# A second level of the 7-for-8 algorithm in the last block's output product, with a GpSimd epsilon and a new order of the lead

## The chip, the cores and the metric

The kernel runs on one core of a Trainium2 chip. Its time is the device time in microseconds (us); before the change it is 1559.0 us, the median of three runs from 1556.36 to 1560.2 us. All profile numbers here are from one profiled execution, whose span is 1553.1 us at a mean granted TensorE clock of 0.998.

## The reference

Attention over 8 batches, 12 heads, 448 positions and 64 dimensions, then a feed-forward layer over the 3584 tokens of 768 features:

```
def rmsnorm(x, g):
    rms = np.sqrt(np.mean(x * x, axis=-1, keepdims=True) + 1e-06)
    return x / rms * g
q_n, k_n = rmsnorm(q, g_q), rmsnorm(k, g_k)
scores = 1.0 / np.sqrt(64) * np.matmul(q_n, k_n.transpose(0, 1, 3, 2))
attn = softmax(scores)                      # exp, divided by the sum over the keys
x = np.matmul(attn, v)                      # to (3584, 768): tokens by heads x dimensions
out = ((x @ w_a) * (x @ w_b)) @ w_out       # w_a, w_b: (768, 1536); w_out: (1536, 768)
```

The three weights arrive as 8-byte floats. The kernel turns them into fp32 itself; everything is then computed in fp32. In the profile one fp32 matmul shows as two records on TensorE (PE) and two weight loads (PEld).

## The kernel before, in words

**Attention.** A step p of 24 covers four heads of one batch (three steps to a batch). It loads q, k and v; squares q and k on ScalarE (L449); sums the squares on VectorE (L451); multiplies by 1/64 and adds 1e-6 on VectorE (L455); raises the result to the power -0.5 on GpSimd (L457); scales q with it (L461); and turns q and k over on TensorE (L487). Then, for seven slices j of the keys, TensorE makes the scores (L508), ScalarE their exponentials (L514), and TensorE multiplies them by v (L530). The sums over the keys: in the first five steps (WIDE) by a matmul with ones for each slice (L566); in the later 19 the seven exponentials are first added up by six additions of 128 x 896 elements (L544), each on the engine that ADD_UP names, and one matmul with ones follows. The sums are inverted through a round trip to DRAM (L586 to L595) and multiplied into the result (L636).

**Feed-forward.** Two batches make a block, so there are four blocks (beta 0 to 3) of 896 tokens. Each of the two layers uses a form of Strassen's algorithm: a product of two 2 x 2 block matrices in 7 block products in place of 8, at the price of additions of blocks. The first layer (`quarter_products`, matmuls at L790) keeps a weight's 7 factors stationary and streams 448 tokens. The second (`last_product`) keeps token tiles stationary and streams 384 columns of a factor of w_out: for each of its 7 products f, in the order 0, 1, 2, 4, 3, 5, 6, and each pair t of token tiles it makes six matmuls of 128 x 384 (`product`, L718). Blocks 0 and 2 have three pairs, blocks 1 and 3 have four (one made of the tiles left over). VectorE makes the sums of token tiles (`sum_`, L706) and adds the products up (L738, L754, L761, L767); `store` (L862) sends finished tiles out from SyncE.

**Weights.** `factors` loads the two parts of a piece of weight (L372, L375, issued by ScalarE's queue), rounds it (L271 to L280), makes the seven factors (L385), and keeps them in DRAM (L393, L396) for the later blocks; `stream` brings them back (L406, L408) into one of two buffers `st`. `weights` calls it for 18 pieces in the order `seq`, each not before the moment in GATES. The five first pieces are of w_out.

**The order of the work.** Everything is recorded first as operations of a `Plan`: engine, an estimated duration, a key (the lower, the more urgent), what it reads and writes, and which buffers it opens. `Plan.run` then simulates the engines with these estimates and writes every engine's instructions in the order that comes out. The order on the chip is therefore fixed; a wait on the chip holds everything behind it on that engine. An operation with `lock=True` is planned so that no two such operations of VectorE and GpSimd overlap. NORM says how many steps ahead of its use a step's normalization is keyed, LANDING what is allowed for a transfer to arrive, XS the number of buffers of 128 x 3 x 448 elements that hold the attention's results and their sums. The lead, as it is called here, is the time until the first block's first layer runs alone, some 240 us, in which attention and weights share all engines.

Of the kernel before, what the change touches and what calls it, by code (L numbers as in the profile page):

```python
# [25 lines left out]
class Plan:  # L26
# [10 lines left out]
    LANES = 8  # L37
    RATE, LANDING = 300.0, 2.0
    STAY = 0.3
# [131 lines left out]
def kernel(  # L171
# [35 lines left out]
    nc = tc.nc  # L207
# [91 lines left out]
    def fast_body(ld, wk, ps_s, ps_o, ps_mm, dram):  # L299
        plan = Plan()  # L300
        op, tile_of = plan.op, plan.tile
        NORM = 2.5
        EARLY = 1.5
        FEW = S // 8
        HC, NT = HP // 2, S // D
        NC = B * HC
        STS, XS = 2, 9
        WARM = 8
        APART = 24
        WIDE = 5  # L310
        ADD_UP = [None, 'DVE', 'POOL', 'DVE', 'POOL', 'DVE', 'DVE']

# [37 lines left out]
        def factors(n, key, early, after):  # L350

            last = n >= len(order)
            st = tile_of(f"st{n}", "st", STS)

            def begin():
                sts[n] = ld.tile([P, 7, KH * P], FP32, tag="st", name="st", bufs=STS)
            op(None, 0.0, key, begin, [], [f"{st}/{x}" for x in range(7)] + ["streaming"], new=[st])
            if last:
                m = n - len(order)
                steps = ((0, 4, 1, 0), (0, 5, 3, 1), (1, 1, 3, 4), (0, 6, 2, 1))  # L360
            else:
                m, ab = order[n]
                src = (moe_w_a, moe_w_b)[ab]
                steps = ((0, 4, 2, 3), (1, 5, 0, 2), (0, 2, 4, 0), (0, 6, 1, 2))
            words, row = place(early)

            for part in range(2):
                def load(part=part):
                    to = words()[:, part * NW:(part + 1) * NW]
                    if last:  # L370
                        k = m + part * MH
                        nc.scalar.dma_start(to, moe_w_out[k * P:(k + 1) * P, :])  # L372
                    else:
                        at = part * HM + m * P
                        nc.scalar.dma_start(to.rearrange("p (k n) -> p k n", k=KA),  # L375
                                            src[:, 2 * at:2 * (at + P)].rearrange("(k p) n -> p k n", p=P))
                op("ACT", 0.45, key - 0.75, load, after, [f"{row}/{part}"], kb=768)
            rounding(key, NW, lambda: (words().rearrange("p (n w) -> p n w", w=2), sts[n][:, 0:4].rearrange("p a b -> p (a b)")),
                     [f"{row}/{part}" for part in range(2)], f"{st}/0")
            homes = [0, 0, 0, 0, 4, 5, 6]  # L380
            for pool_, to, x, y in steps:
                add = to == 4 and not last
                e = FACTOR if pool_ else "DVE"
                op(e, 1.05 if e == "POOL" else 0.6, key,
                   lambda e=e, to=to, x=x, y=y, add=add: two[e].tensor_tensor(  # L385
                    sts[n][:, to], sts[n][:, x], sts[n][:, y], ALU.add if add else ALU.subtract),
                   [f"{st}/{homes[x]}", f"{st}/{homes[y]}"], [f"{st}/{homes[to]}"], lock=True)

            def keep():
                if last:  # L390
                    if "o" not in kept:
                        kept["o"] = dram.tile([P, 7, MH, HALF], FP32, name="kept_o")
                    nc.scalar.dma_start(kept["o"][:, :, m], sts[n])  # L393
                else:
                    kept[n] = dram.tile([P, 7 * KH * P], FP32, name=f"kept{n}")
                    nc.scalar.dma_start(kept[n], sts[n].rearrange("p a b -> p (a b)"))  # L396
            op("ACT", 0.45, key, keep, [f"{st}/{x}" for x in range(7)], [f"kept{n}"], kb=1376)

# [33 lines left out]
        def normalize(p):  # L432
# [8 lines left out]
            def squares(s, nm):  # L441
                sq = tile_of(f"sq{nm}{p}", "sq", 1)

                def square():
# [3 lines left out]
                            x.rearrange("p j h d -> p (j h) d"))  # L448
                    nc.scalar.activation(t, flat, AF.Square)  # L449
                op("ACT", 1.07, key, square, [f"{nm}{p}"], [sq], new=[sq])  # L450
                op("DVE", 1.1, key, lambda: nc.vector.tensor_reduce(rs[p][:, s], xs["sq", nm, p], AX, ALU.add), [sq], [f"{ms}/{nm}"])  # L451

            def roots(a, b, names):
                msf = lambda: rs[p][:, a:b].rearrange("p s n -> p (s n)")
                op("DVE", 0.2, key, lambda: nc.vector.tensor_scalar(msf(), msf(), 1.0 / D, 1e-6, ALU.mult, ALU.add), [], names)  # L455
                op("POOL", 2.7 if b - a == 1 else 5.0, key,
                   lambda: nc.gpsimd.tensor_tensor(msf(), msf(), expo[:, 0:2 * NT * (b - a)], ALU.pow), [], names)  # L457

# [111 lines left out]
        def invert(p):  # L570
# [25 lines left out]
            for w in range(2):  # L596
                op("ACT", 0.55, p - 0.5, lambda w=w: move(w), [f"su{p}.{w}" if p < WIDE else f"su{p}"], [t], new=[t] if w == 0 else [])
            op("SP", 0.8, p - 0.0, spread_out, [t], [few], new=[few], kb=20, dmas=2)
            op("DVE", 0.3, p - 0.0, lambda: nc.vector.reciprocal(fews[0], fews[0]), [], [few])
            op("SP", 0.4, p - 0.0, leave, [few], [f"inv{p}"], kb=20)  # L600
            op("SP", 1.0, p - 0.0, come_back, [f"inv{p}"], [t], kb=460, dmas=2)

# [13 lines left out]
        def put_out(p):  # L616

            for w in range(2):
# [4 lines left out]
                def take(w=w, x=x, c=c):  # L623
                    if c == 0:
                        quads[x] = wk.tile([P, KH, S], FP32, tag="x", name="x", bufs=XS)
                    nc.scalar.copy(quads[x][:, c], os_[p][:, w, 0:S])
                op("ACT", 0.55, p, take, [f"o{p}"], [f"{x}/{c}"] + (["quarter"] if c == 0 else []), new=[x] if c == 0 else [])

        def divide(p):

            for w in range(2):
                x, c = home(p, w)

                def emit(w=w, x=x, c=c):
                    t = quads[x][:, c]
                    nc.vector.tensor_tensor(t, t, sus[p][:, w], ALU.mult)  # L636
                op("DVE", 0.65, p, emit, [f"rec{p}"], [f"{x}/{c}"], lock=True)

# [6 lines left out]
        def combine(beta, c):  # L645

            B11, B21, B12, B22, T2, T3, T4 = names_of(beta)
            for to, x, y in ((T3, B22, B12), (B12, B12, B11), (T2, B22, B12), (T4, B21, T2)):
# [6 lines left out]
                if first:  # L655
                    tile_of(to, "x", XS)
                op("DVE", 0.63, -0.5, emit, [f"{x}/{c}", f"{y}/{c}"], [f"{to}/{c}"] + (["quarter"] if first else []),
                   new=[to] if first else [], lock=True)
# [20 lines left out]
        def last_product(beta, h, key):  # L679
# [24 lines left out]

            def sum_(to, x, y, alu):
                op("DVE", 0.98, -0.5, lambda: nc.vector.tensor_tensor(to[0](), x[0](), y[0](), alu), x[1] + y[1], to[1][:1], lock=True)  # L706

# [21 lines left out]
            def out_(t, i, x, y):  # L729

                g = 2 * S * beta + (t + OWN * i) * P if t < OWN else 2 * S * (beta - 1 + i) + 2 * OWN * P

# [10 lines left out]
            for f in (0, 1, 2, 4, 3, 5, 6):  # L743
                stream(beta, 12 + place_of[f], f)
            for t in pairs:
                sum_(n_(t), A(1, 0, t), A(1, 1, t), ALU.add)
                sum_(n_(t), n_(t), A(0, 0, t), ALU.subtract)
            for t in pairs:
                product(t, 0, A(0, 0, t), lambda po, ps, t=t: op(
                    "ACT", 0.5, -1, lambda: nc.scalar.copy(acc(t, 0), ps()), [po], [c_(t)]))  # L750
                sum_(A(0, 0, t), A(0, 0, t), A(1, 0, t), ALU.subtract)
            for t in pairs:
                product(t, 1, n_(t), lambda po, ps, t=t: op(
                    "DVE", 0.6, -1, lambda: nc.vector.tensor_tensor(acc(t, 1), acc(t, 0), ps(), ALU.add), [po, c_(t)], [U_(t)]))  # L754
            for t in pairs:
                product(t, 2, A(0, 1, t), out_(t, 0, 0, 0))
                sum_(A(0, 1, t), A(0, 1, t), n_(t), ALU.subtract)
                sum_(n_(t), A(1, 0, t), A(1, 1, t), ALU.add)
            for t in pairs:
                product(t, 4, n_(t), lambda po, ps, t=t: op(  # L760
                    "DVE", 0.6, -1, lambda: nc.vector.tensor_tensor(acc(t, 0), acc(t, 1), ps(), ALU.add), [po, U_(t)], [c_(t)]))  # L761
            for t in pairs:
                product(t, 3, A(0, 1, t), out_(t, 0, 1, 0))
            for t in pairs:
                def both(po, ps, t=t):
                    out_(t, 1, 1, 0)(po, ps)
                    op("DVE", 0.6, -1, lambda: nc.vector.tensor_tensor(acc(t, 1), acc(t, 1), ps(), ALU.add), [po], [U_(t)])  # L767
                product(t, 5, A(0, 0, t), both)
            for t in pairs:
                product(t, 6, A(1, 1, t), out_(t, 1, 0, 1))  # L770
            if not odd:
                op("ACT", 1.5, 0, lambda: nc.scalar.copy(left(), H()[:, :, 2 * OWN * P:]), allh, [f"{fin}/left"])

        def quarter_products(beta, key, m, ab, st, at, names, h):
# [112 lines left out]

        GATES = [0, 2, 4, 4, 5, 5, 7, 7, 8, 8, 10, 10, 16, 18, 21, 21, 27, 32]
        seq = [15, 13, 16, 12, 14, 0, 1, 2, 3, 4, 5, 6, 7, 8, 9, 10, 11, 17]
        def weights(at, after):  # L890
            for x, n in enumerate(seq):
                if at == GATES[x]:
                    factors(n, x * 0.45 + 1.0, x < 2, [after])

# [4 lines left out]
        for p in range(NC + 1):  # L899
# [16 lines left out]
            if p > 0:  # L916
# [6 lines left out]
                if p % (2 * HC) == 0:  # L923
                    combine(p // (2 * HC) - 1, 1)
                    combine(p // (2 * HC) - 1, 2)
                    ffn(p // (2 * HC) - 1)
            if p < NC:
# [139 lines left out]
```

## Time and profile before

| engine | busy, us | share of the span | what it mostly does |
|---|---|---|---|
| PE | 1518.8 | 98% | first layer (L790) 763.2, second layer (L718) 388.4, the rest attention |
| DVE (VectorE) | 715.0 | 46% | weights, sums, taking products from PSUM |
| ACT (ScalarE) | 395.7 | 25% | exponentials 192.2 |
| POOL (GpSimd) | 313.6 | 20% | power 146.3, products of the first layer 86.2, adding up 80.9 |

An engine's busy time is a sum over its records; matmuls overlap in the records, so the mean of a record (540 ns for 448 columns) is a latency, and the distance between two of them is read from a run of many: their time divided by their number. Shares over the whole span hide where an engine is short, so the table is read together with a table by stage, in which each row is a stretch of the span.

### The profile page before, as it was taken

The page shows a single profiled execution, that of the slowest core. Times are in us where ns is not written, and L with a number is a line of the kernel's source. Part 1 is how long each engine was busy: PE and PEld are TensorE (multiplying, and loading weights), DVE is VectorE, ACT ScalarE, POOL GpSimd, SP SyncE. Part 2 cuts the span into 40 slices and gives each one's busy share as a digit, 9 for nine tenths or more (in the row PEclk, how much of TensorE's full clock was granted, in tenths as well). Part 3 has the DMA queues.
Part 4 walks back from the last instruction along what each step waited for, and adds up shares of the span by engine and source line. Part 5 has one row for each costly group of instructions (what it writes and reads, how often), then busy time and mean ns, then how long its engine had stood idle before and what let it go on. Part 6 is the DMA issues. An engine that isn't in the chain of part 4 may idle for free.

```text
span 1553.1 us, 16949 instructions
## 1 busy us (share of the span) xinstructions
PE 1518.8 (98%) x6714; PEld 790.3 (51%) x6714; DVE 715.0 (46%) x932; ACT 395.7 (25%) x637; POOL 313.6 (20%) x166
## 2 busy tenths in 40 slices
PE   8988999999999999999999999999999999999998
PEld 6653345555444555555444555555545555555554
DVE  4887869888786412222476421222245221222421
ACT  5767661111567200000547300000040000000000
POOL 3416542211345200011246200001010001001000
PEclk9999999999999999999999999999999999999999
DMA  9897445544445542212325333222213422121222
GB/s 248 234 264 228 97 108 176 210 171 169 146 118 126 152 147 75 103 71 106 91 80 127 89 118 117 100 78 85 92 44 117 156 90 107 72 107 66 95 92 80
DMA packets 113884, 192.26 MB, mean 124 GB/s; under 512 B 56196, under 2 KB 99460, under 8 KB 104068
## 3 DMA queue, kind: packets, MB, share of 16 engines
q1 hardware_dynamic: 86052, 138.00, 30.2%
q10 hardware_dynamic: 27744, 53.09, 9.8%
q8 instruction: 55, 0.90, 0.2%
q14 instruction: 33, 0.27, 0.1%
HBM read 154.93 MB, written 35.95 MB: 123 GB/s over the span
## 4 chain that ended last, share of the span: by engine, by line
PE 88%; DMA 4%; ACT 3%; DVE 3%; issue 1%; POOL 1%; SPq 0%; ACTq 0%; DVEq 0%; POOLq 0%
PE pq L790 48%; PE po L718 24%; PE sc L508 6%; PE o L530 6%; PE pt L487 2%; PE su L566 2%; ACT ET L514 2%; DMA q_sb<-in_q_dram 1%; DMA kept_o<-st 1%; PE warm L879 1%; DMA hraw<-in_moe_w_out_dram 1%; DVE x L636 0%; DVE sum L544 0%; DMA st<-kept_o 0%; DMA rec<-inv 0%
## 5 line engine op out<-in xcount | busy, mean ns | idle before, releaser
L790 PE MATMUL pq<-x,st 128*128 128x448 f32 x2016 | 763.2, 540 | 0.0
L790 PEld LDWEIGHTS pq<-x,st 128*128 128x128 f32 x2016 | 382.2, 190 | 377.4 <-issue 369.9
L718 PE MATMUL po<-st,hT 128*128 128x384 f32 x744 | 244.0, 487 | 0.0
L514 ACT ACTIVATE ET<-sc,ms 128x448 f32<-128x448 f32 x336 | 192.2, 635 | 89.8 <-PE sc L508 64.2
L530 PE MATMUL o<-ET,v_sb 64*64 64x448 f32 x1344 | 184.7, 547 | 8.2 <-ACT ET L514 7.7
L508 PE MATMUL sc<-qkT 64*64 64x448 f32 x1344 | 176.5, 546 | 16.5 <-ACT ET L514 8.3
L718 PEld LDWEIGHTS po<-st,hT 128*128 128x128 f32 x744 | 141.0, 190 | 100.6 <-issue 3.6
L457 POOL TENSOR_TENSOR ms<-ms,expo 128x14 f32<-128x14 f32 x48 | 146.3, 3051 | 190.6 <-DVE ms L455 185.7
L838 POOL TENSOR_TENSOR hT<-hT,t 128x448 f32<-128x448 f32 x24 | 28.4, 1184 | 756.1 <-DVE t L836 753.9
L718 PE MATMUL po<-st,fin 128*128 128x384 f32 x432 | 144.4, 489 | 0.0
L812 ACT COPY hT<-pq 128x448 f32<-128x448 f32 x24 | 12.8, 532 | 441.7 <-PE pq L790 441.7
L718 PEld LDWEIGHTS po<-st,fin 128*128 128x128 f32 x432 | 81.2, 190 | 61.4 <-issue 6.3
L544 POOL TENSOR_TENSOR sum<-sum,ET 128x896 f32<-128x896 f32 x38 | 80.9, 2130 | 129.8 <-ACT ET L514 74.8
L508 PEld LDWEIGHTS sc<-qkT 64*64 64x64 f32 x1344 | 58.7, 133 | 92.6 <-issue 33.7
L530 PEld LDWEIGHTS o<-ET,v_sb 64*64 64x64 f32 x1344 | 60.0, 133 | 85.6 <-ACT ET L514 40.6
L738 DVE TENSOR_TENSOR o_sb<-fin,po 128x384 f32<-128x384 f32 x56 | 31.0, 554 | 155.9 <-PE po L718 155.9
L544 DVE TENSOR_TENSOR sum<-sum,ET 128x896 f32<-128x896 f32 x57 | 62.4, 1094 | 39.2 <-POOL sum L544 30.8
L850 POOL TENSOR_TENSOR hT<-hT,t 128x448 f32<-128x448 f32 x48 | 57.8, 1206 | 49.5 <-DVE t L847 45.9
L451 DVE TENSOR_REDUCE ms<-sq 128x14 f32<-128x896 f32 x48 | 51.8, 1078 | 25.0 <-ACT sq L449 25.0
L843 DVE TENSOR_TENSOR hT<-U,pq 128x448 f32<-128x448 f32 x48 | 29.8, 621 | 66.0 <-PE pq L790 66.0
L815 ACT COPY t<-pq 128x448 f32<-128x448 f32 x24 | 12.8, 533 | 176.0 <-PE pq L790 176.0
L847 DVE TENSOR_TENSOR t<-U,pq 128x448 f32<-128x448 f32 x48 | 29.7, 619 | 60.1 <-PE pq L790 57.8
(69 smaller groups left out, 923.0 us busy)
## 6 DMA issues: line engine op xcount, KB each, us to landing
st<-kept SPq DMA_DIRECT2D x36, 1344.0 KB
st<-kept_o SPq DMA_DIRECT2D x28, 1152.0 KB
kept<-st ACTq DMA_DIRECT2D x12, 1344.0 KB
q_sb<-in_q_dram SPq DMA_DIRECT2D x48, 224.0 KB
k_sb<-in_k_dram SPq DMA_DIRECT2D x48, 224.0 KB
v_sb<-in_v_dram SPq DMA_DIRECT2D x48, 224.0 KB
rec<-inv SPq DMA_DIRECT2D x48, 224.0 KB
out_dram<-o_sb SPq DMA_DIRECT2D x112, 96.0 KB
```

Source lines behind the costliest of these rows:

```text
L451: op("DVE", 1.1, key, lambda: nc.vector.tensor_reduce(rs[p][:, s], xs["sq", nm, p], AX, ALU.add), [sq], [f"{ms}/{nm}"])
L457: lambda: nc.gpsimd.tensor_tensor(msf(), msf(), expo[:, 0:2 * NT * (b - a)], ALU.pow), [], names)
L487: nc.tensor.transpose(t[:, j * P:(j + 1) * P], x[:, j].rearrange("p h d -> p (h d)"), ident)
L508: nc.tensor.matmul(t[low_high[w], e, 0:S], lhsT=qkTs[p][low_high[e], 1, j * P + w * D:j * P + (w + 1) * D], rhs=qkTs[p][low_high[e], 0, w ...
L514: nc.scalar.activation(E[:, e], scs[p, j][:, e, 0:S], AF.Exp, scale=rs[p][:, 1, 2 * j + e:2 * j + e + 1])
L530: nc.tensor.matmul(os_[p][low_high[e], w, 0:S], lhsT=xs["v", p][low_high[w], e, j * D:(j + 1) * D], rhs=ETs[p, j][low_high[w], e], start=( ...
L544: two[e].tensor_tensor(sums[p], sums[p] if j > 1 else ETs[p, 0], ETs[p, j], ALU.add)
L566: nc.tensor.matmul(sus[p][w][low_high[e], :], lhsT=ones[low_high[w], :], rhs=x[low_high[w], e], start=first, stop=last)
L718: nc.tensor.matmul(held["po"][:, 0:HALF], lhsT=a[0]()[:, c], rhs=sts[beta, 12 + place_of[f]][:, c], start=(c == 0), stop=(c == MH - 1))
L738: nc.vector.tensor_tensor(held["o"], acc(t, y), ps(), ALU.add)
L790: nc.tensor.matmul(banks[bank][:, 0:S], lhsT=sts[at][:, f, c * P:(c + 1) * P], rhs=quads[x][:, c], start=(start and c == 0), stop=(stop an ...
L850: lambda i=i, n=n, nm=nm: two[TIMES].tensor_tensor(C(i, n), C(i, n), held[nm], ALU.mult), [t], [hp[i]],
```

## The change

It has four parts.

- **Second level.** In the last block alone (ONCE), for five of the seven products (TWICE: f = 1, 2, 3, 4, 6), two pairs of token tiles are taken together as a 2 x 2 block matrix, and their product with the factor of w_out is done in 7 products of three matmuls of 128 x 192 where the plain form takes 12 matmuls of 128 x 384, the work of 8 such products (`inner_products`). The factors of the factors are made once, in block 1 (MAKE), by VectorE, and kept in DRAM (`inner_factors`); in the last block they are read back into buffers that the finished attention no longer needs (`stream_inner`). Products 0 and 5 stay plain. The sums of token tiles that the last block needs first are made piece by piece while its first layer still runs.
- **1e-6 on GpSimd.** The squares are scaled on ScalarE so that their sum is the mean; the addition of 1e-6 moves from VectorE to GpSimd, ahead of the power.
- **Adding up.** ADD_UP gives four of the six additions to GpSimd, where it was two.
- **Order of the lead.** Loads of weights are issued by SyncE (LOADS) in place of ScalarE; keys, GATES, `seq`, NORM, LANDING and some estimated durations change, and XS goes from 9 to 8.

```diff
-    RATE, LANDING = 300.0, 2.0
+    RATE, LANDING = 300.0, 2.5
...
-        NORM = 2.5
+        NORM = 2.0
...
-        STS, XS = 2, 9
+        STS, XS = 2, 8
         WARM = 8
+        TWICE = (1, 2, 3, 4, 6)
+        MAKE = 1
+        ONCE = NB - 1
+        LOADS = "SP"
+        KEEPS = "ACT"
...
-        ADD_UP = [None, 'DVE', 'POOL', 'DVE', 'POOL', 'DVE', 'DVE']
+        ADD_UP = [None, 'DVE', 'POOL', 'POOL', 'DVE', 'POOL', 'POOL']
...
-                        nc.scalar.dma_start(to, moe_w_out[k * P:(k + 1) * P, :])
+                        queue[LOADS].dma_start(to, moe_w_out[k * P:(k + 1) * P, :])
...
-                op("ACT", 0.45, key - 0.75, load, after, [f"{row}/{part}"], kb=768)
+                op(LOADS, 0.45, key - 2.0, load, after, [f"{row}/{part}"], kb=768)
...
-                    nc.scalar.activation(t, flat, AF.Square)
+                    nc.scalar.activation(t, flat, AF.Square, scale=float(D) ** -0.5)
...
-                op("DVE", 0.2, key, lambda: nc.vector.tensor_scalar(msf(), msf(), 1.0 / D, 1e-6, ALU.mult, ALU.add), [], names)
-                op("POOL", 2.7 if b - a == 1 else 5.0, key,
-                   lambda: nc.gpsimd.tensor_tensor(msf(), msf(), expo[:, 0:2 * NT * (b - a)], ALU.pow), [], names)
+
+                def root():
+                    nc.gpsimd.tensor_scalar(msf(), msf(), 1e-6, None, ALU.add)
+                    nc.gpsimd.tensor_tensor(msf(), msf(), expo[:, 0:2 * NT * (b - a)], ALU.pow)
+                op("POOL", 3.2 if b - a == 1 else 5.6, key, root, [], names)
...
+            def each(f, a, base, to):
+                twice = groups if f in TWICE else []
+                for g in twice:
+                    inner_products(beta, key + place_of[f], f, g, a, base, to, acc, (c_, U_), out_place)
+                for t in pairs if not twice else alone:
+                    product(t, f, a(t), plain(t, base, to))
...
+            factor(0, a10, a11, ALU.add, nx1)
+            factor(1, s(0), a00, ALU.subtract, nx0 + [f"{S_}/0"])
+            factor(2, a00, a10, ALU.subtract, nx)
+            factor(3, a01, s(1), ALU.subtract, nx0 + [f"{S_}/1"])
...
+            product("a", a00, b_quarter(0, 0), nx0 + [st], True, False)
+            op("ACT", 0.32, -1, copy, [bank_of["a"]], [f"{t_}/0"], new=[t_])
+            product("b", s(1), b_made(1), [f"{S_}/1", f"ti{beta}.{f}.1"], True, True)
...
+            product("a", a01, b_quarter(1, 0), nx0 + [st], False, True)
...
+            product("d", s(0), b_made(0), [f"{S_}/0", f"ti{beta}.{f}.0"], True, True)
...
+            product("g", s(2), b_made(2), [f"{S_}/2", f"ti{beta}.{f}.2"], True, False)
...
+            product("e", s(3), b_quarter(1, 1), [f"{S_}/3", st], True, True)
+            product("g", a11, b_made(3), nx1 + [f"ti{beta}.{f}.3"], False, True)
...
-        GATES = [0, 2, 4, 4, 5, 5, 7, 7, 8, 8, 10, 10, 16, 18, 21, 21, 27, 32]
-        seq = [15, 13, 16, 12, 14, 0, 1, 2, 3, 4, 5, 6, 7, 8, 9, 10, 11, 17]
+        GATES = [0, 2, 3, 4, 5, 6, 7, 7, 7, 9, 11, 11, 11, 11, 17, 17, 18, 20]
+        seq = [13, 15, 12, 14, 16, 0, 1, 2, 3, 4, 5, 6, 7, 8, 9, 10, 11, 17]
...
-                    factors(n, x * 0.45 + 1.0, x < 2, [after])
+                    factors(n, x * 0.65 + 0.5, x < 1, [after])
```

## The prediction

> **What bounds the kernel now.** First the page: busy time by engine, and the line of the 40 slices for TensorE.
>
> ```profile
> PE 1518.8 (98%) x6714; PEld 790.3 (51%) x6714; DVE 715.0 (46%) x932; ACT 395.7 (25%) x637; POOL 313.6 (20%) x166
> ...
> PE   8988999999999999999999999999999999999998
> ```
>
> TensorE is the bound, and only the first four slices and the last show room. The view by windows says how much:
>
> ```profile
> 0.00:240.00 240.00, 217.78 (x1796) 120.20 (x1797) 179.54 (x216) 159.55 (x250) 104.99 (x44) 0.99 0.73 194
> ...
> 380.00:520.00 140.00, 136.55 (x953) 62.99 (x952) 101.61 (x122) 82.75 (x136) 59.85 (x26) 1.00 0.48 128
> ...
> 700.00:875.00 175.00, 172.91 (x1049) 80.89 (x1048) 90.87 (x115) 82.14 (x139) 63.67 (x29) 1.00 0.36 99
> ...
> 1438.00:1547.00 109.00, 108.60 (x337) 63.81 (x335) 33.95 (x49) 1.91 (x4) 1.13 (x1) 1.00 0.30 93
> 1547.00:1553.10 6.10, 0.00 (x0) 0.00 (x0) 0.19 (x1) 0.00 (x0) 0.00 (x0) 0.66 0.15 38
> ```
>
> The columns after the length are PE, PEld, DVE, ACT and POOL busy, then the clock. PE idles 22.2 us in the lead (240 - 217.8), 3.5 and 2.1 us in the attention of blocks 1 and 2, nothing in the last product (from 1438), and 6.5 us in the tail. So a matmul removed from the last product is worth its whole time, and the rest of the change can bring at most the 22 us of the lead. The chain of waits, in order of time (start, length, what), gives the price of a matmul:
>
> ```profile
> 12.61 9.43 DMA hraw<-in_moe_w_out_dram
> ...
> 25.12 1.12 PE o L530 x5
> ...
> 193.60 1.53 PE pt L487 x14
> ...
> 958.15 178.14 PE pq L790 x474
> ...
> 1438.24 108.37 PE po L718 x336
> ```
>
> A record of 384 columns comes every 108.37 / 336 = 322.5 ns, one of 448 every 178.14 / 474 = 375.8 ns, one of 128 (the turning of q and k) every 1.53 / 14 = 109 ns: about 0.83 ns a column and no floor down to 128. The first two lines belong to the lead: a piece of w_out, loaded by ScalarE's queue at 12.6, holds ScalarE, and TensorE's next product waits until 25.1. Last, the groups (busy us, mean ns | idle before them):
>
> ```profile
> L457 POOL TENSOR_TENSOR ms<-ms,expo 128x14 f32<-128x14 f32 x48 | 146.3, 3051 | 190.6 <-DVE ms L455 185.7 <-ACT x L626 4.1
> L718 PEld LDWEIGHTS po<-st,hT 128*128 128x128 f32 x744 | 141.0, 190 | 100.6 <-issue 3.6 <-DVE sum L544 0.7 <-DVE o_sb L738 0.7
> ...
> L544 POOL TENSOR_TENSOR sum<-sum,ET 128x896 f32<-128x896 f32 x38 | 80.9, 2130 | 129.8 <-ACT ET L514 74.8 <-DVE sum L544 38.8 <-DVE ms L451 11.8
> L544 DVE TENSOR_TENSOR sum<-sum,ET 128x896 f32<-128x896 f32 x57 | 62.4, 1094 | 39.2 <-POOL sum L544 30.8 <-ACT ET L514 7.3
> ...
> L455 DVE TENSOR_SCALAR ms<-ms 128x14 f32<-128x14 f32 x48 | 18.6, 388 | 1.4
> ```
>
> GpSimd takes 1.95 times as long as VectorE for the same addition.
>
> **What the Trainium skill says.** "TensorE: Matmul & The Clock Gate", section "LDWEIGHTS (loading the stationary operand)": a load takes its columns / 1.2 ns, so 107 ns for 128, whatever the rows. The trace shows records of 190 ns but turnings with a load each every 109 ns, so 190 is a latency, and a load fits under 192 columns. The same page, Part 1: after about 3.4 us of idleness the clock is halved until TensorE has been busy again. The trace agrees: after the gap up to 25.1 the granted clock is 0.83 in 24 to 28 us and 0.74 in 28 to 32. "SBUF — State Buffer", "SBUF: two separate sides": VectorE operations with two SBUF inputs and GpSimd operations take one pair of ports by an exclusive lock. The 0.388 us of L455, whose shortest is 0.110 and longest 2.092, fit an operation held by GpSimd.
>
> **Second level, TensorE.** Ten groups (five products, two groups each) lose 12 matmuls of 384 columns, 240 records in all: 240 x 322.5 ns = 77.4 us. They gain 21 of 192, 420 records. At the line through 128 and 384 (109 and 322.5 ns: 0.834 a column) a record is 162.4 ns: 68.2 us. **Gain 9.2 us** (an eighth of 77.4 would be 9.7; the fixed part of more records takes the rest). The bounds: 320/2 = 160 ns with no fixed part gives 10.2; if the 190 ns of a load did bind, 420 x 190 = 79.8, a loss of 2.4. I take 162, since the 109 ns speak against the second.
>
> **Second level, VectorE.** A group takes four sums of 384 elements (L385 has this shape: 0.55 undisturbed), six additions out of PSUM of 192 (384 take 0.555, 448 0.62, so about 0.36) and two on SBUF (0.35 and 0.55): 2.2 + 2.2 + 0.9 = 5.3 us, beside 6.8 us of TensorE (42 x 162 ns). The stage has 33.6 us of VectorE work in 108; it gets 53 more and loses 20 additions of 0.555, 11: some 75 in 99 us. It stays hidden on average. Locally it may not: between f = 2 and f = 4 lie eight sums of 0.96 (L706) and the eight factors of f = 4, 12 us, while TensorE has 13.7 us of f = 2, whose own additions take another 6 us of VectorE. Each group's first and third products need no such factor (2 us of cover), so I put 1 us for stalls, between 0 and 4. Sums moved under the first layer cost nothing: VectorE is busy 71 of 268 us there (1170 to 1438). Making 20 factors of 576 elements (0.75) costs 15 us of VectorE in block 1, busy 58 of 255 us there, and 5.9 MB out and back over queues at a DMA share of 0.3: hidden. The tail stays DVE, then two transfers; two tiles now end 1 us apart rather than 3.9, and a pair of issues takes 1.1 us (1547.2 to 1548.3): +0.5, between 0 and 1.
>
> **1e-6.** It takes 48 operations of 0.388 from VectorE, 18.6 us and one hand-over of each chain, and puts 48 on GpSimd. No such row exists there; setting 28 columns takes 0.12 us (L236), selecting over 128 columns 0.29: between 0.12 and 0.5, I take 0.3. Behind it in GpSimd's order wait the power and the additions; for the power wait q's scaling and then the turning on TensorE. The scale on ScalarE is free, being part of the same activation.
>
> **Adding up.** Nineteen steps move two additions each: VectorE loses 2 x 1.09, GpSimd gains 2 x 2.13. A step of TensorE is 7.35 (scores) + 7.70 (values) + 1.90 (turning) + 1.0 (sums), 18 us; GpSimd goes from 2 x 3.05 + 2 x 2.13 = 10.4 to 15.2 us of it. That fits, with 15% to spare. The chain of six additions grows from 8.6 to 10.7 us, under 18. I put 1 us for attention, between -3 and 19.
>
> **Order of the lead.** Moving loads to SyncE frees ScalarE of 10 issues of about 0.4 us in the lead, and the first piece of w_out is issued right behind the first v, some 5 us earlier. The gap before 25.1 is 3.9 us, and the slow clock behind it costs 8 us x 0.21 = 1.7; I take 60% of these 5.6. The other 18 us are small waits for ScalarE, with VectorE busy 75%; relief of VectorE (18.6 us of L455 over 24 steps, some 8 in the lead) may take a tenth, 2 us. With XS = 8 the first layer of block 0 begins after 9 steps, not 11; that moves work, not its sum. **Gain 5 us**, between -6 and 14: SyncE's queue is in order too, and a load that waits for room holds q and k of the next step.
>
> **Sum.** 1559.0 - 9.2 + 1 + 0.5 + 1 - 5 = 1547.3, say 1547.
>
> **Rivals.** (A) The lead clears more than I allow: half of its 22 us and the slow clock, 12 us in place of 5, and no stalls: 1559 - 9.2 + 0.5 - 12 = 1538. For it: the gap has one visible cause. Against: DMA share is near 1 from 20 to 140 us, and the order alone moves no fewer bytes. (B) The second level is partly eaten: stalls of 4 us in the last product, tail +1, lead and attention together nothing: 1555. For it: VectorE would be over TensorE at f = 2 to 4. Against: two banks and two pairs of banks let TensorE run ahead. (C) GpSimd becomes the bound of attention. With the port lock, two-input work of VectorE (two additions, q's scaling, dividing, block sums: about 6 us a step) must fit into the gaps of 8.5 us of GpSimd additions; a late sum holds TensorE, whose order is fixed. One us a step is 19 us, no gain in the lead, stalls as forecast: 1559 - 9.2 + 2.5 + 19 = 1571, slower than before. For it: 85% busy leaves little for an in-order queue, and VectorE now waits for GpSimd on more links. Against: powers last 3 us but VectorE's two-input L278 ran at its usual 1.76 us beside one at 29.6, so they don't hold the port.
>
> **Numbers.** Forecast 0.52, A 0.18, B 0.18, C 0.12. The range leaves out C and the far side of A: 1536 to 1560. Faster than 1554.3: forecast, A and half of B, 0.79; within 0.3%: the other half of B and little else, 0.09; slower: C, 0.12.
>
> **What would show it.** In the second profile: records of 192 columns every 162 ns in the chain (near 190 would refute the main step); PE busy about 1510; idle of PE in the last product under 4 us; a first gap of PE shorter than 3.9 us and a clock of 1.00 at 24 to 32 us; the sum's matmul with ones not waiting on GpSimd L553's additions. PE idle above 15 us between the lead and the last block would mean C.

## The result, and the profile after

The changed kernel takes 1576.16 us (median of 4 runs), the kernel before 1557.83 us beside it: a ratio of 1.0116, 95% interval 1.0098 to 1.0134. It is **slower by 18 us**, where 1547 was forecast. The two profiled executions lie 22.6 us apart (1575.7 against 1553.1), since that of before took less than its median and that of after more. The accounts below are in profile time, so about 4 us in them are scatter between executions.

The page of the kernel after, busy time by engine and TensorE's line of slices:

```profile
PE 1522.8 (97%) x6894; PEld 819.0 (52%) x6894; DVE 729.3 (46%) x982; ACT 399.0 (25%) x647; POOL 430.4 (27%) x252
...
PE   9888799999999999999999999999999999999987
```

The last but one slice is no longer full, and one at 160 us is a 7. By windows (stretch, length, busy PE, PEld, DVE, ACT, POOL, granted clock, DMA share, GB/s), kernel after:

```profile
0.00:240.00 240.00, 212.62 (x1579) 119.41 (x1580) 166.57 (x184) 137.30 (x211) 120.62 (x69) 0.96 0.67 195
380.00:520.00 140.00, 137.31 (x889) 65.70 (x882) 80.56 (x91) 75.92 (x125) 97.51 (x50) 1.00 0.50 136
700.00:875.00 175.00, 173.22 (x1055) 85.57 (x1054) 94.00 (x108) 82.60 (x139) 99.22 (x53) 1.00 0.42 120
1450.50:1568.00 117.50, 104.82 (x516) 85.60 (x515) 64.94 (x144) 5.12 (x14) 1.13 (x1) 1.00 0.36 115
```

Three readings. The lead idles 27.4 us where it idled 22.2, and its clock is 0.96, not 0.99. The attention of blocks 1 and 2 idles 2.7 and 1.8 us: as little as before (3.5 and 2.1), with GpSimd busy 97.5 of 140 us and 99.2 of 175. The last product, which had no gap, now has 12.7 us of them (117.5 - 104.8). The chain of waits of the kernel after, around the end of the last first layer (start, length, what):

```profile
1261.07 189.42 PE pq L986 x504
...
1450.49 15.48 PE po L729 x48
1465.97 2.92 PE ab L903 x18
1468.89 1.96 PE dg L903 x12
1471.29 1.26 PE dg L903 x6
1472.98 1.24 PE dg L903 x6
1474.22 2.92 PE ab L903 x18
...
1566.64 1.26 PE dg L903 x6
```

These lines cut the loss in three. The last product begins at 1450.5 where it began at 1438.2: **12.3 us lost ahead of it**. On TensorE it lasts 117.4 us (1450.5 to 1567.9) and not 108.4: **9.0 us lost in it**, where 8.2 were to be gained. The tail grows from 6.5 to 7.8: 1.3. Together 22.6. The first part is the one that scatters: two runs below, e1 and e4, have the order of this kernel ahead of the last product, and in their profiles it begins 8.7 and 7.6 us later than before, not 12.3.

A third view says where the first part arises. The end of each block's first layer, read from the chain, gives these lengths (us):

| kernel | start to block 0 | to block 1 | to block 2 | to block 3 | rest |
|---|---|---|---|---|---|
| before | 386.1 | 364.7 | 385.5 | 301.9 | 114.9 |
| after | 371.4 | 362.1 | 386.2 | 330.8 | 125.2 |

### The profile page after: what moved, and what is told of

It reads as the page before. It is cut to its first block, busy times and chain, and to the rows that moved or that the text cites. A ratio compares the mean times of both kernels' runs of the same rounds, so it can differ in the third digit from the quotient of the medians.

```text
span 1575.7 us, 17582 instructions
## 1 busy us (share of the span) xinstructions
PE 1522.8 (97%) x6894; PEld 819.0 (52%) x6894; DVE 729.3 (46%) x982; ACT 399.0 (25%) x647; POOL 430.4 (27%) x252
## 4 chain that ended last, share of the span: by engine, by line
PE 90%; DVE 3%; DMA 3%; ACT 2%; issue 1%; SPq 0%; POOL 0%; ACTq 0%; DVEq 0%; POOLq 0%
PE pq L986 49%; PE po L729 19%; PE o L539 7%; PE sc L517 6%; PE dg L903 3%; PE su L575 2%; PE pt L496 2%; PE ab L903 2%; ACT ET L523 1%; DMA kept_o<-st 1%; DMA rec<-inv 1%; PE warm L1075 1%; DVE fin L716 1%; DVE x L646 1%; DMA few<-rec 1%
## 5 line engine op out<-in xcount | busy, mean ns | idle before, releaser
L729 PE MATMUL po<-st,hT 128*128 128x384 f32 x624 | 206.7, 488 | 0.0
L553 POOL TENSOR_TENSOR sum<-sum,ET 128x896 f32<-128x896 f32 x76 | 165.8, 2181 | 140.9 <-DVE sum L553 115.7
L539 PE MATMUL o<-ET,v_sb 64*64 64x448 f32 x1344 | 191.1, 547 | 6.3 <-ACT ET L523 5.7
L729 PEld LDWEIGHTS po<-st,hT 128*128 128x128 f32 x624 | 117.2, 190 | 86.9 <-issue 7.3
L465 POOL TENSOR_TENSOR ms<-ms,expo 128x14 f32<-128x14 f32 x48 | 140.3, 2922 | 4.0
L729 PE MATMUL po<-st,fin 128*128 128x384 f32 x312 | 104.0, 488 | 0.0
L729 PEld LDWEIGHTS po<-st,fin 128*128 128x128 f32 x312 | 58.6, 190 | 44.2 <-issue 3.5
L749 DVE TENSOR_TENSOR o_sb<-fin,po 128x384 f32<-128x384 f32 x44 | 24.4, 555 | 107.0 <-PE po L729 101.1
L464 POOL TENSOR_SCALAR ms<-ms 128x14 f32<-128x14 f32 x48 | 36.7, 765 | 116.3 <-DVE ms L458 114.3
```

The source lines that it names most:

```text
L464: nc.gpsimd.tensor_scalar(msf(), msf(), 1e-6, None, ALU.add)
L539: nc.tensor.matmul(os_[p][low_high[e], w, 0:S], lhsT=xs["v", p][low_high[w], e, j * D:(j + 1) * D], rhs=ETs[p, j][low_high[w], e], start=( ...
L553: two[e].tensor_tensor(sums[p], sums[p] if j > 1 else ETs[p, 0], ETs[p, j], ALU.add)
L729: nc.tensor.matmul(held["po"][:, 0:HALF], lhsT=a[0]()[:, c], rhs=sts[beta, 12 + place_of[f]][:, c], start=(c == 0), stop=(c == MH - 1))
```

## Experiments

Differences in us are (ratio - 1) x 1558. Every run was timed beside the kernel before on the same chip, whose medians were 1557.2 to 1558.8. Theory names (X, Q, R, T and others) are those of the expectations.

### Which half costs

**e1** keeps the lead and attention as changed and has no second level:

```
-        TWICE = (1, 2, 3, 4, 6)
-        ONCE = NB - 1
+        TWICE = ()
+        ONCE = NB
```

> The changed kernel without the second level (TWICE empty, ONCE past the last block): the last product is plain again and nothing is made in block 1. Read from the two traces, the first layer of the last block ends 12.3 us later than before, and the last product with its tail takes 10.3 us more. Theory L (the lead's order alone costs the 12.3): 1566 to 1571 us, the first layer of the last block ending near 1450, the last product back at 108.4 us. Rival (making the inner factors and moving sums cost time before the last product): about 1558 us, the end of the first layer near 1438.

Measured 1568.74, ratio 1.0060 (1.0043 to 1.0078), +9 us. **e2** is the opposite: second level and XS = 8 kept, everything else of the lead and attention as before (loads on ScalarE's queue, 1e-6 on VectorE, ADD_UP, keys, GATES and `seq`).

> The kernel before plus the second level alone; XS is 8 as in the change (9 leave no room in SBUF for the two tk buffers). Orders, keys, loads, 1e-6 and adding up are as before. Theory L: the lead is as before, only the last product is longer: 1558 + 10 = 1568 us. Rival X (XS = 8 is what costs the lead its 12 us): 1580 us, the first layer of the last block ending near 1450.

Measured 1573.7, 1.0090 (1.0068 to 1.0112), +14. **e3** is the kernel before with one number changed:

```
-        STS, XS = 2, 9
+        STS, XS = 2, 8
```

> The kernel before with XS = 8 in place of 9 and nothing else. Theory L: within 3 us of 1558. Rival X: 1570 us.

Measured 1566.48, 1.0052 (1.0025 to 1.0078), +8. So the second level costs about 7 us in the old order (1573.7 - 1566.5) and 7.5 in the new one (1576.2 - 1568.7). Both halves lose, and within the intervals they add up. The lengths of e3 are 362.7, 363.4, 387.6, 332.8: two attention steps move from the lead to the stretch before the last first layer. They were worth 23.4 us in the lead (386.1 - 362.7) and cost 30.9 us behind it (332.8 - 301.9). Why they cost more there is not shown: TensorE idles in that stretch no more than before (0.2 us against 0.1).

### Why the second level costs

In the chain above a group of 42 matmul records of 192 columns takes 8.25 us (1465.97 to 1474.22), while 18 records in 2.92 us are 162 ns each, so that 42 need 6.8. The group's products are called a, b, d, e and g in the code, after the PSUM region they go to; a and g are each made of two products of three matmuls that add up. The timeline of the kernel after in one group (start, length, engine, line, what, in brackets the idle time before and who ended it):

```profile
1468.73 2.11 PE L903 MATMUL dg<-ti,Si 128*128 128x192 f32 x12
...
1470.88 0.35 DVE L946 TENSOR_TENSOR pi<-pi,dg 128x192 f32<-128x192 f32 x1 [1.59 <-PE dg L903]
...
1471.29 1.24 PE L903 MATMUL dg<-st,Si 128*128 128x192 f32 x6 [0.45 <-DVE pi L946]
...
1472.57 0.35 DVE L955 TENSOR_TENSOR fin<-pi,dg 128x192 f32<-128x192 f32 x1 [0.35 <-PE dg L903]
...
1472.98 0.43 PE L903 MATMUL dg<-ti,fin 128*128 128x192 f32 x1 [0.45 <-DVE fin L955]
```

The 12 records are d (six) and the first half of g (six); d alone is done after six records, yet VectorE takes it (L946) only at 1470.88, when both are. The product e, written into the same tile `dg`, waits for that (1471.29). VectorE takes the first half of g (L955) only at 1472.57, when e is done, and the second half of g, which adds onto the first, waits for L955. **e4** gives d, g and e a tile each, from PSUM that attention has left by then (excerpt; the lines that open the tiles follow suit):

```
-            dg = tile_of(f"dg{id_}", "sc", 2)
+            dg = tile_of(f"g{id_}", "sc", 2)
-            bank_of = {..., "d": f"{dg}/d", "e": f"{dg}/e", "g": f"{dg}/g"}
+            bank_of = {..., "d": tile_of(f"d{id_}", "sc", 2), "e": tile_of(f"e{id_}", "o", 1), "g": dg}
```

> The changed kernel with d, g and e of each group in three PSUM tiles of their own (two of the score tiles and the result tile, all idle by then) where d, e and g shared one. In the changed kernel VectorE takes d up only when the first g has ended too, e waits for that, and the second g waits for VectorE: 0.60 + 0.71 us of bubble a group, ten groups. Theory S (the shared tile makes both waits): the bubbles nearly vanish, the last product goes from 117.4 to about 104 us, 1562 us in all. Rival D (VectorE's chain of dependent additions is what TensorE waits for, whatever the banks): no change, 1574 to 1576 us.

Measured 1564.59, 1.0041 (1.0031 to 1.0050): 11.6 us faster than the kernel after. The same group in the timeline of e4:

```profile
1464.11 2.12 PE L904 MATMUL dg<-ti,Si 128*128 128x192 f32 x12
...
1465.29 0.35 DVE L947 TENSOR_TENSOR pi<-pi,dg 128x192 f32<-128x192 f32 x1 [0.62 <-PE dg L904]
...
1466.06 1.14 PE L904 MATMUL eo<-st,Si 128*128 128x192 f32 x6
...
1467.13 0.95 PEld L904 LDWEIGHTS dg<-ti,fin 128*128 128x128 f32 x6 [0.23 <-DVE fin L956]
1467.13 1.24 PE L904 MATMUL dg<-ti,fin 128*128 128x192 f32 x6
```

VectorE takes d right after its own six records and the first half of g while e runs; e follows without a wait, and TensorE's waits inside this group are gone. A group now takes 7.03 us. The arithmetic then closes. A plain group is 24 records of 322.5 ns, 7.74 us. At 8.25 the second level loses 0.51 a group, 5.1 us in ten. The other 3.9 of the 9.0 measured are in single groups that take longer than 8.25: 3.0 of them in the two groups where f = 2 gives way to f = 4 (1490.99 to 1510.48), with a wait of 2.08 us at 1498.92 for L959 and one of 1.80 at 1502.94 for L877. A wait costs more than its idle time: six records last 1.26 us behind one in the chain and 0.97 where e runs on without one (e18, below). So against the 6.8 us a group, 18 us are lost in all, of which 12.7 are gaps. At 7.03 it gains 0.71 a group, 7.1 us.

### Why the lead costs

The first suspect was XS, since e3 alone gave +8. **e5** is e1 with XS = 9:

```
-        STS, XS = 2, 8
+        STS, XS = 2, 9
```

> The changed kernel without the second level, and with XS = 9 again, so the new order of the lead, 1e-6 on GpSimd and the new adding up alone. Theory X (XS = 8 puts two attention steps behind the lead, where they cost TensorE 15 us each, and shortens the lead by only 12 each; the other parts cancel): 1559 us, the first layer of the last block ending within 4 us of 1438. Rival O (the new order itself costs what the run without the second level lost): 1567 to 1569 us.

Measured 1573.88, 1.0100 (1.0071 to 1.0130), +16: in the new order XS = 8 saves some 5 us (the two intervals just overlap). Theory X falls for the new order. **e6** is e1 with the loads back on ScalarE's queue (`LOADS = "ACT"`, key - 0.75):

> The changed kernel without the second level and with the loads of weights on ScalarE's queue again, keyed as before (XS = 8). In the changed kernel's trace a round trip of the inverted sums waits for its transfer from 98.4 to 107.9 us in SyncE's own queue, and TensorE waits for it 3.4 us and runs slow afterwards. Theory Q (loads of weights on SyncE's queue delay the round trip): the first layer of block 0 ends near 363, as with the old order, not 367 to 371; some 1564 us. Rival (keys and gates of the lead are the cause): no change from 1568.7.

Measured 1584.96, 1.0178 (1.0151 to 1.0206), +28: theory Q falls too. With the loads on its queue ScalarE is later than in e1, where the same row reads 6.5 us in total, 7 times, longest 2.0; TensorE's waits of e6 (for whom, us in total, times, longest) up to 400 us:

```profile
PE o L539 <- ACT ET L523: 15.6, 8, 4.9
```

**e7** is e1 with the old ADD_UP (`'DVE', 'POOL', 'DVE', 'POOL', 'DVE', 'DVE'`):

> The changed kernel without the second level and with two of the six additions on GpSimd again in place of four (XS = 8). Rival C of the prediction (GpSimd with four additions is the bound of attention): faster by up to 19 us. Theory: from the end of block 0's first layer to the end of block 3's the changed kernel took 890 us and the old order with XS = 8 894 us, so four additions on GpSimd cost nothing: within 4 us of 1568.7.

Measured 1573.93, 1.0096 (1.0063 to 1.0128), +15, if anything 5 slower than e1 (the intervals overlap). More additions on GpSimd are no burden there, which leaves little of rival C.

Then each other part was taken out of e5, one at a time. **e9**: 1e-6 and the scale back on VectorE (the lines of the diff reversed).

> The new order of the lead without the second level at XS = 9 (1573.9 us), with the factor 1/64 and the 1e-6 on VectorE again. On GpSimd the addition took 0.77 us on average, up to 1.7, where 0.3 had been put; it stands between the squares and the power. Theory E (this lengthens the chain that q's scaling waits for, and so the lead): 1564 to 1568 us, the first layer of block 0 ending some 6 to 10 us before 400. Rival (the chain has room; keys or gates): no change beyond 3 us.

Measured 1575.84, 1.0111 (1.0093 to 1.0130). **e10**: old GATES, `seq` and keys of `factors`.

> The same base (1573.9 us) with GATES, the order of the pieces and their keys as before (0.45 a piece from 1.0, two pieces into the early place), still loaded by SyncE. Theory G (the thinner spread of the pieces, 0.65 of a step each, leaves weight work for the time when TensorE could run the first layer, and is what costs the 14 us): the first layer of block 0 ends near 386, 1558 to 1562 us. Rivals E and K (1e-6; keys of the round trip, NORM, LANDING): no change beyond 3 us.

Measured 1573.28, 1.0098 (1.0081 to 1.0116). **e11**: old keys of the sums' round trip (`p - 0.0` in place of `p - 2.0`), NORM, LANDING and estimates.

> The same base (1573.9 us) with the keys of the round trip of the inverted sums, NORM, LANDING and the estimated durations of dividing and combining as before. Theory K (the round trip, keyed two steps early, and the later normalization hold SyncE's queue and VectorE): 1560 to 1566 us. Rivals E and G: no change beyond 3 us.

Measured 1571.57, 1.0086 (1.0069 to 1.0102). None of the three is more than 2.3 us from e5: none of these parts, taken out alone, gives the loss back.

What do the gaps look like? In the lead of the kernel after, 105 to 110 us, timeline:

```profile
107.87 1.16 DVE L646 TENSOR_TENSOR x<-x,rec 128x448 f32<-128x448 f32 x2 [4.21 <-DMA rec<-inv]
109.07 0.97 ACT L588 COPY rec<-su 128x448 f32<-128x448 f32 x2 [4.63 <-DVE x L646]
...
109.65 1.45 PE L575 MATMUL su<-ET,ones 64*64 64x448 f32 x4 [3.44 <-ACT rec L588]
```

Read upwards: TensorE waits for ScalarE's copy of sums into the one buffer `rec`, the copy for VectorE's division (a product with the inverted sums) that still reads `rec`, the division for the transfer that brings the inverted sums back. Windows of 4 us of the same kernel show what follows such a gap (PE busy first, clock after POOL):

```profile
108.00:112.00 4.00, 2.35 (x14) 1.57 (x18) 3.62 (x6) 1.01 (x3) 0.08 (x1) 0.56 0.63 198
112.00:116.00 4.00, 4.00 (x30) 2.60 (x26) 0.00 (x0) 3.67 (x5) 0.00 (x0) 0.59 0.67 204
```

The granted clock is 0.56 and 0.59 for 8 us. "TensorE: Matmul & The Clock Gate" of the Trainium skill has it slow after about 3.4 us of idleness (Part 1), and the gap here is 3.44. Summed over 4-us windows up to 240 us as busy time x (1 - clock), the slow clock costs 7.2 us after and 1.5 before. With the idle time that is 5.2 + 5.7 = 10.9 of the 12.3 us.

How much of this is the order, and how much one execution? In the profiles of e1 and e4 VectorE, GpSimd and SyncE run the same operations in the same order through the lead. The same gap is 2.18 and 2.51 us long there, and the first window behind it reads, e1 and then e4:

```profile
108.00:112.00 4.00, 4.00 (x30) 2.66 (x30) 1.61 (x4) 1.87 (x5) 0.00 (x0) 0.63 0.57 161
108.00:112.00 4.00, 3.91 (x42) 2.08 (x46) 2.05 (x4) 2.87 (x7) 0.00 (x0) 1.00 0.67 229
```

So a gap of 2.18 us was followed by a slow clock as well, against the page's 3.4, and one of 2.51 by none. Idle time up to 240 us is 27.2 and 26.5 us in these two, and the slow clock costs 4.2 and 4.3: with 22.2 and 1.5 before, that is 7.7 of the 8.7 us of e1 and 7.1 of the 7.6 of e4. Idle time and clock account for nearly all of the loss in all three executions; some 8 us of it belong to the order, and the rest of the 12.3 to this one execution.

Theory R said that the single buffer makes these gaps. **e12**, the kernel before with XS = 8 (e3) and a second `rec`:

```
-    fews["rec"] = wk.tile([P, 2, S], FP32, tag="rec", name="rec")
+    fews["rec"] = wk.tile([P, 2, S], FP32, tag="rec", name="rec", bufs=2)
```

> The kernel before with XS = 8 (1566.5 us) and two buffers rec for the sums over the keys in place of one. In the kernel before each of the first five steps copies its sums only after the step before has divided by its own (81.8 after 80.7, 106.5 after 105.4, 134.0 after 132.8), 20 to 27 us apart where TensorE needs about 18 to 25. Theory R (this single buffer and the round trip behind it set the pace of the lead): the lead loses most of its 22 us of idle TensorE, 1552 to 1558 us. Rival (transfers and VectorE set it): within 3 us of 1566.5.

Measured 1571.17, 1.0091 (1.0072 to 1.0109): 6 us slower than e3, where theory R has it 9 to 14 faster. R falls as a forecast; since the planner's order changed with the buffers, what the second one is worth in an unchanged order was not seen. There the lead idles 28.7 us and loses 8.7 to the clock, where e3 has 22.3 and 2.8: more room, another order from the planner, a worse lead. That suggested theory T: any edit draws a new fixed order. It was put to the test by single parts put into the kernel before, XS = 9, no second level. **e13**: the loads on SyncE, key - 2.0.

> The kernel before (XS = 9, old order) with one part of the change: the loads of weights issued by SyncE, keyed two steps ahead. Theory Q (sharing SyncE's queue with q, k, v and the round trip is what costs): 1565 to 1575 us. Rival F (it removes the first gap of 3.9 us and the slow clock after it): 1552 to 1555 us. If any disturbance of the old order costs (theory T): 1565 or more, too, but the same holds for the other three parts.

**e14**: 1e-6 on GpSimd.

> The kernel before with the scale in ScalarE's square and the 1e-6 on GpSimd alone. Theory E (0.77 us more on GpSimd in each normalization lengthens the lead): 1562 to 1568 us. Rival (VectorE's 18.6 us of L455 are saved, the chain has room): 1554 to 1558 us. Theory T: 1565 or more.

**e15**: the new ADD_UP.

> The kernel before with four of the six additions on GpSimd alone. At XS = 8 in the new order taking this back cost 5 us, so: 1553 to 1557 us; rival C (GpSimd is the bound of attention): 1565 to 1575 us. Theory T: 1565 or more.

**e16**: the new GATES, `seq` and keys of `factors`.

> The kernel before with the new GATES, order of pieces and their keys alone (loads still from ScalarE's queue). Theory G (the thinner spread of the pieces costs the lead): 1565 to 1575 us. Rival: within 4 us of 1558. Theory T: 1565 or more.

| run | median | ratio (95%) | us | start to block 0 | to block 1, 2, 3 | idle to 240 | lost to the clock |
|---|---|---|---|---|---|---|---|
| before | 1557.65 | | | 386.1 | 364.7, 385.5, 301.9 | 22.2 | 1.5 |
| e13 loads | 1564.71 | 1.0043 (1.0026 to 1.0060) | +7 | 397.3 | 364.7, 385.8, 302.0 | 27.1 | 3.4 |
| e14 1e-6 | 1571.36 | 1.0089 (1.0069 to 1.0108) | +14 | 405.3 | 359.3, 387.8, 303.8 | 28.7 | 5.6 |
| e15 adding up | 1573.81 | 1.0104 (1.0087 to 1.0120) | +16 | 403.1 | 363.1, 388.5, 302.1 | 28.0 | 5.3 |
| e16 gates | 1569.52 | 1.0084 (1.0065 to 1.0103) | +13 | 396.5 | 368.0, 385.5, 301.9 | 25.9 | 3.0 |

Each alone costs 7 to 16 us, where all together (e5) cost 16, and most of it lies before the end of block 0's first layer. About half of the growth there is idle time and slow clock up to 240 us; the rest was not traced. In e15 that also answers rival C, whose 1565 to 1575 us it hits: the stretches to blocks 1 to 3, where 13 of the 19 steps that add up run, change by -1.6, +3.0 and +0.2 us. Nor did the part miss its aim: in e13 the gap of 20 to 40 us shrinks from 3.9 to 0.5 us, and its stretch still grows by 11. One gap of e15 shows the kind of thing that a new order brings, timeline at 171 to 177 us:

```profile
171.36 0.62 DVE L645 TENSOR_TENSOR x<-x,rec 128x448 f32<-128x448 f32 x1 [2.19 <-DMA rec<-inv]
172.02 2.60 DVE L663 TENSOR_TENSOR x<-x 128x448 f32<-128x448 f32 x4
174.53 0.62 DVE L645 TENSOR_TENSOR x<-x,rec 128x448 f32<-128x448 f32 x1
...
175.23 0.97 ACT L587 COPY rec<-su 128x448 f32<-128x448 f32 x2 [0.99 <-DVE x L645]
...
176.25 1.02 PE L516 MATMUL sc<-qkT 64*64 64x448 f32 x4 [4.08 <-ACT rec L587]
```

Between the two divisions that free `rec` the order has put four block sums (L663), 2.6 us; ScalarE's copy stands behind the second, and TensorE's scores wait 4.08 us for the copy. This fits T. So does e13, which moves only loads: VectorE scales q (L469, at 26.68) ahead of L278 (27.68) there, and behind it in the old order (L461 at 31.27, L278 at 29.60). And e16 costs as much as the others, though it moves no work from one engine to another. But T is argued and not shown: 1564.7 (e13) lies just under the 1565 it named, e15 and e16 also hit the ranges of the theories of their own parts, and an edit with no aim at all, a few keys shifted at random, was not tried. What stays open is why the order before is so much better than every new one: the gaps come at other places in each, and no rule was found that tells a good order from a poor one ahead of a run. The round trip's new keys were not tried alone in the old order.

### What the second level is worth in the old lead

**e8**: old order and XS = 9, the second level with the tiles of e4; the inner factors are made in halves, in the buffers `t`, so that they need no room of their own and XS can stay at 9.

> The kernel before, with XS = 9 and all its orders, plus the second level with d, g and e in PSUM tiles of their own; the factors of the factors are made in halves in the tiles t of the first layer, so that no tk buffers are needed and XS = 9 fits. Theory: lead as before (end of the last first layer near 1438), the last product with its tail 113 us as with own banks, where it was 115: 1557 us. If making the factors in halves (40 operations of VectorE, 40 small transfers) disturbs block 1: 1560 or more.

Measured 1556.17, 0.9995 (0.9986 to 1.0004): no difference from before. Its last stage takes 112.2 us, against 114.9, and the stretch to block 3's first layer 303.8 against 301.9 (so too in e17 and e18); TensorE's longest wait left, 1.8 us, is for VectorE, which has the sums of whole tiles for f = 4 to make right behind those of f = 2. **e17** parts those two: f = 2 runs ahead of f = 1, with the sums between them moved along.

```
-            for f in (0, 1, 2, 4, 3, 5, 6):
+            for f in (0, 2, 1, 4, 3, 5, 6):
```

> As e8 (old lead, XS = 9, own PSUM tiles; 1556.2 us), and the products in the order 0, 2, 1, 4, 3, 5, 6, so that VectorE makes four of the eight sums that f = 4 needs during f = 1 rather than between f = 2 and f = 4. In e8 the two groups of f = 2 and the start of f = 4 took 3 + 2 us more than the others. If these sums are the wait: 1551 to 1553 us, the last product near 101 us. If the eight sums only move the wait: 1556.

Measured 1552.63, 0.9967 (0.9958 to 0.9975). **e18** adds room for the finished tiles on their way out, since a store of 8.15 us stands in the chain of e4 ahead of a plain product, which waits 0.8 us for a tile to fill:

```
-   o_of[x] = ld.tile([P, HALF], FP32, tag="o_sb", name="o_sb")
+   o_of[x] = wk.tile([P, KH, S], FP32, tag="x", name="oi", bufs=XS).rearrange("p a b -> p (a b)")[:, 0:HALF]
```

> As e17, and the finished groups go out from buffers of the attention's results, idle by then, in place of the two buffers o_sb. In e8 the second group of f = 3 and the following plain product waited some 2 us behind a store of 5.7 us. If that is a wait of its own: 1 to 2 us less than e17, 1550 to 1552; the whole gain over the kernel before would then be some 6 to 7 us of the forecast 9.2. If the store is hidden: as e17.

Measured 1551.4, 0.9963 (0.9948 to 0.9977): the fastest, 6 us below before, though the step from e17 is within the interval. One group in its chain, and its last two stretches by windows:

```profile
1485.81 2.92 PE ab L909 x18
1488.73 1.95 PE dg L909 x12
1490.68 0.97 PE eo L909 x6
1491.65 1.18 PE dg L909 x6
1492.83 2.92 PE ab L909 x18
```

```profile
1441.90:1543.90 102.00, 101.65 (x516) 85.87 (x515) 65.33 (x144) 5.12 (x14) 1.13 (x1) 1.00 0.42 132
1543.90:1551.20 7.30, 0.00 (x0) 0.00 (x0) 0.35 (x1) 0.00 (x0) 0.00 (x0) 0.67 0.28 63
```

The group takes 7.02 us, the last product 102.0 us, 6.4 less than before, of the 7.1 that ten groups of 7.03 allow; the tail takes back 0.8.

## Why the prediction was wrong

- **Second level on TensorE, gain 9.2:** right in its price (162 ns a record, 18 in 2.92 us), and a load does fit under 192 columns.
- **Stalls, 1 us, bounds 0 to 4: the first step that failed.** They came to 9.0 + 9.2 = 18 us. The working looked for them where VectorE is overloaded, between f = 2 and f = 4; those came, about 3 us beyond an ordinary group. The larger part is in each of the ten groups: 8.25 us against 6.8, 14 us in all. Rival B's "two banks and two pairs of banks let TensorE run ahead" counted tiles and did not ask which products share one: d, e and g do, and VectorE took d only when the g behind it was done. `inner_products` names that tile in one line; e4 shows its price, 11.6 us. VectorE's average load, 64.9 us of 117.5, was rightly seen as no limit.
- **Lead, gain 5, bounds -6 to 14: the second step that failed.** It lost 12.3 in the profile after, 8.7 and 7.6 in e1 and e4: in each more than the 6 that the lower bound allowed. The named gap did go: 20 to 40 us now idles 1.4 us at a clock of 1.00, where it idled 3.9 at 0.91. The error was to take a fixed order as if removing one gap left the rest in place: e13 to e16 show that four parts, each alone, cost 7 to 16 us, most of it there. Why every new order is worse stays open.
- **"XS = 8 ... moves work, not its sum": failed.** The two steps are 23.4 us in the lead and 30.9 behind it in the old order (e3); in the new order the exchange seems to pay (e1 against e5). So it wasn't free, and its price depends on the order.
- **1e-6 on GpSimd, 0.3 us, at most 0.5: too small.** The group line of the kernel after (busy, mean ns, idle before it):

```profile
L464 POOL TENSOR_SCALAR ms<-ms 128x14 f32<-128x14 f32 x48 | 36.7, 765 | 116.3 <-DVE ms L458 114.3
```

  The mean is 765 ns, the shortest 258. The Trainium skill, "Perfetto Trace Analysis", section "GPSIMD Engine Instruction", warns that spans on this engine are unreliable; here it makes no difference to the verdict, since taking the part out of e5 moves +2 us (e9, within the intervals). In the old order the part came with +14 (e14), far more than its own time.
- **Attention, 1 us, and rival C: right.** The stretches to block 1 and block 2 changed by -2.6 and +0.7 us, and the sums' matmul does not appear among TensorE's waits for GpSimd. But the 15% to spare were not there: 18 us a step is a sum of records that overlap, and two steps packed together took 30.9 us (e3), 15.5 each, beside the 15.2 forecast for GpSimd. What kept GpSimd from binding, as far as the windows show it, is that attention is mixed with other products: in block 1 GpSimd was busy 97.5 of 140 us. The slower side, on which C lay, came true, but by another way than the one named for it.
- **Tail, 0.5, at most 1:** 1.3.
- **Signs named ahead:** 162 ns a record and a first gap shorter than 3.9 us at a clock of 1.00 came true. TensorE's busy time is 1522.8 us, where about 1510 was named, and its idle time in the last product 12.7, where under 4 was.

In the sum: stalls and gain of the last product 17.2 us off, lead and attention together 16.3 (12.3 lost, 4 gained in the forecast), tail 0.8. That is the 34.3 us between the forecast of -11.7 and the 22.6 of the profile; by the medians the loss is 18.3 and the distance 30.

## What to carry to other kernels

Before pricing a shorter product by its matmuls, list which results share a tile, and ask of each reader how many later writes it will wait for: 1.2 us a group turned a gain of 0.71 into a loss of 0.51. Where the order of all engines is simulated and then fixed, do not price an edit in a crowded stage by the gap it aims at; give such an edit a range as wide as that stage's whole idle time, on both sides, and test each part alone in the old order. This rests on the runs of one kernel. And a tuned stage is better left as it is when a change elsewhere can be fitted into the room there is: e17 and e18, the two versions faster than before, keep the old lead.

## What the runs showed of the hardware

A read by VectorE of one part of a shared PSUM tile began after the later writes to another part had ended (1470.88 in the kernel after), and with a tile for itself right after its own (1465.29 in e4); the profile reads the ends of these waits from semaphores, which points to the waits that the program sets for a whole tile, but it was not measured apart from the memory. An addition of a constant to 128 x 14 elements on GpSimd ranged from 258 to 1735 ns, and the power right behind it from 2610 to 4628. A gap of TensorE of 3.44 us cost most of its length again in slow clock: at 0.56 with 2.35 us busy and 0.59 with 4.00 us, 2.7 us. Behind a gap of 2.18 us at the same place (e1) the clock was 0.63 for one window of 4 us, behind one of 2.51 (e4) it stayed at 1.00.

In the kernel before, VectorE's addition of 1e-6 (L455, one input, 128 x 14) has a median of 0.17 us. But the one at 191.47 lasts 2.09, until 193.56, beside an addition on GpSimd (L544) from 191.44 to 193.53; the one at 131.93 lasts 0.98, until 132.91, and GpSimd's addition ends at 132.89. Five more of 1.2 to 2.1 us (165.42, 185.50, 443.39, 492.47, 868.45) end with one of GpSimd's in the same way. So the small operation is held until GpSimd's addition ends, and part of the 18.6 us that the prediction took off VectorE was waiting.
